# Scaling e in place of v^T e: the softmax factor in an attention and two-layer FFN kernel

## The chip, the cores and the metric

The kernel runs on one core of a Trainium2 chip. The metric is the device time of one execution in microseconds (us); the time before is the median of three runs. The profile is one further execution, taken by the hardware profiler.

## The reference, cut to what matters

All tensors are float32. The attention has 4 batches of 8 heads, 576 positions and a head size of 64:

```
scores = (q @ k^T) / 8
thresh = max(scores) - tau                       # per row
scores = where(scores >= thresh, scores, -1e9)
attn   = exp(scores - max(scores))
attn   = attn / (sum(attn) + 1e-9)               # per row
x      = attn @ v                                # heads joined: 2304 x 512
h      = ((x @ w1) * (x @ w2)) @ w3 @ w_out      # first FFN, 2304 x 512
g      = leaky_relu(h @ w_in, 0.01)              # 2304 x 2048
out    = g @ moe2_w_out                          # 2304 x 512
```

The change is to the line with the division by the sum.

## The kernel before, in words

The attention works on units: one pair of heads and one group of query rows. Group g=0 holds 256 query rows of the pair in two steps, g=1 holds 320 in three; a step is 128 rows of both heads, except the first of g=1, which takes the last 64 rows of both heads as one tile of 128. A batch is four units g=0 and then four units g=1; there are 32 units and 80 steps, and 64 of the steps hold two tiles of scores (128 query rows by 576 keys), 16 hold one.

A step goes through three functions. `scores` multiplies q by k into PSUM (tile sc), takes the row maximum on VectorE (nm) and writes e = exp(sc - max) on ScalarE. `mask` keeps e where the score is above the threshold, on VectorE (SCALAR_TENSOR_TENSOR), and gives the row sums in the same instruction (tile stat). `transposes` turns e on TensorE into PSUM (tp and, for the last 64 keys, tq) and copies it out to HH and tl. When a unit's steps are through, `weighted` multiplies v by HH and tl into a PSUM tile av: x transposed (64 numbers of each head of the pair in 128 partitions, query rows in the columns), without the division. ScalarE copies av to xs.

The query rows stand in the columns of av but in the partitions of the row sums. So `reciprocals` takes 1/(sum + 1e-9) on VectorE, GpSimd writes each factor 64 times side by side (rb), and `normalise` turns rb on TensorE into a PSUM tile bc (two transposes, and in g=1 one product more with the constant `pairs`), multiplies xs by bc on VectorE, and splits the result into a high part (ScalarE, rounded to the type fp32r) and a low part (GpSimd, the rest): x, the input of the first FFN. Products of the FFN take three passes over such parts.

The loop over steps n issues mask(n), scores(n+1), weighted of the unit before where one has just ended, and transposes(n), with pieces of other TensorE work in between: at first the folding of w3 and w_out (`fold_weights`, tile ps), later the first FFN of the queries that are through (`gated`: tiles psab, at, gt, psh), with 256 columns beside the g=1 units of the same batch and 320 beside the g=0 units of the next. `normalise` of a unit came in the second step of the next unit. Beside the first steps the weights are decoded from 64-bit words on ScalarE, VectorE and GpSimd (`stream`: tiles raw, t, lw). Behind the attention comes the second FFN, from about 650 us on.

TensorE's order and that of the DMA queue SP are as written in the code; ScalarE, VectorE and GpSimd are ordered by a scheduler, which also gives out the buffers of the pools. Pool ps_w has two PSUM banks, for av, bc, ps, psab, psh; sc0, sc1, tp and tq have one buffer each, and so a score tile must be masked before the next scores of that head can be computed.

Of the kernel before, what the change touches and what calls it, by code (L numbers as in the profile page):

```python
# [8 lines left out]
F32 = mybir.dt.float32  # L9
F32R = mybir.dt.float32r  # L10
# [3 lines left out]
ALU = mybir.AluOpType  # L14
# [29 lines left out]
def attention_gated_ffn(ctx: ExitStack, tc: tile.TileContext, qkv, tau, w3t, wout, w12, w2, out):  # L44
# [8 lines left out]
    def f(ap):  # L53
        return ap.bitcast(F32)
# [14 lines left out]

    ident = cpool.tile([P, P], F32, name="ident")  # L70
    make_identity(nc, ident)
    pairs = cpool.tile([P, D], F32, name="pairs")
    nc.vector.tensor_tensor(out=pairs, in0=ident[:, :D], in1=ident[:, D:], op=ALU.add)
    sides = cpool.tile([P, P], F32, name="sides")
    nc.vector.memset(sides, 0.0)
    nc.vector.memset(sides[:D, :D], 1.0)
    nc.vector.memset(sides[D:, D:], 1.0)
    qz = [apool.tile([P, P], F32, name=f"qz{i}") for i in range(2)]
    tl = [apool.tile([P, 2, 320], F32, name=f"tl{i}") for i in range(2)]
    for t in (*qz, *tl):  # L80
# [1 line left out]
    qzs = [apool.tile([P, 2, P], F32R, name=f"qzs{i}") for i in range(2)]  # L82
    for t in qzs:
        nc.vector.tensor_copy(t, tl[0][:, :, :P])
    one = cpool.tile([P, 1], F32, name="one")
    nc.vector.memset(one, 1.0)
    tauc = cpool.tile([P, 1], F32, name="tauc")
    neg = cpool.tile([P, 1], F32, name="neg")
    scl = cpool.tile([P, 1], F32, name="scl")
# [145 lines left out]
                    nc.vector.tensor_copy(qzs[u % 2][r, i, r], part[r, S:S + D])  # L235


    sc_t, e_t, stat = {}, {}, {}

    def scores(n):  # L240

# [34 lines left out]
    def mask(n):  # L276
        pair, g, c = STEPS[n]
        sc, ths = sc_t.pop(n)
        key = (pair, g)
        if key not in stat:  # L280
            stat[key] = apool.tile([P, 5], F32, tag="stat", name="stat", bufs=4)
        for a, th in enumerate(ths):
            ev = e_t[n][a].rearrange("p (a b) -> p a b", a=2)
            o = 4 if c is None else 2 * (c % 2) + a
            nc.vector.scalar_tensor_tensor(  # L285
                out=ev, in0=sc[a][:, :, :HS], scalar=th, in1=ev, op0=ALU.is_ge, op1=ALU.mult,
                accum_out=stat[key][:, o:o + 1])

    he_t = {}

# [32 lines left out]
                nc.scalar.copy(tail[D:, :, o:o + P], tq[D:])  # L323
            yield

    xs_t, x_t, rb_t = {}, {}, {}

    def weighted(pair, g):

        gw = GROUPS[g][1]  # L330
        vv = vv_t[units.index((pair, g))]
        HH, tail = he_t.pop((pair, g)), tl[pair % 2]
        av = ps_w.tile([P, 512], F32, tag="w", name="av")
        for i in range(NK):
            for a in (1, 0):
                kc = (4, 0, 1, 2, 3)[i]
                rhs = (HH[:, kc, a] if kc < 4 else tail[:, a])[:, :gw]
                nc.tensor.matmul(  # L338
                    av[a * D:a * D + D, :gw], vv[:, a, kc], rhs, start=(i == 0), stop=(i == NK - 1))
        xs = apool.tile([P, 320], F32, tag="xs", name="xs", bufs=2)  # L340
        nc.scalar.copy(xs[:, :gw], av[:, :gw])
        xs_t[pair, g] = xs

    def reciprocals(pair, g):

        st = stat.pop((pair, g))
        n = 4 + g
        rr = apool.tile([P, 5], F32, tag="rr", name="rr", bufs=2)
        nc.vector.tensor_scalar(out=rr[:, :n], in0=st[:, :n], scalar1=1e-9, scalar2=None, op0=ALU.add)
        nc.vector.reciprocal(rr[:, :n], rr[:, :n])  # L350
        rb = apool.tile([P, 3, P], F32, tag="rb", name="rb")
        nc.gpsimd.tensor_tensor(
            out=rb[:, :2].rearrange("p c (h d) -> p (c h) d", h=2),
            in0=rr[:, :4].unsqueeze(2).to_broadcast([P, 4, D]),
            in1=one.unsqueeze(2).to_broadcast([P, 4, D]), op=ALU.mult)
        if g:
            nc.gpsimd.tensor_tensor(
                out=rb[:, 2], in0=rr[:, 4:5].to_broadcast([P, P]), in1=sides, op=ALU.mult)
        rb_t[pair, g] = rb

    def normalise(pair, g):
        gq, gw, cs = GROUPS[g]
        xs, rb = xs_t.pop((pair, g)), rb_t.pop((pair, g))
        bc = ps_w.tile([P, 512], F32, tag="w", name="bc")
        if g:
            nc.tensor.matmul(bc[:, :D], rb[:, 2], pairs, start=True, stop=True)
        for i, c in enumerate(cs):
            nc.tensor.transpose(bc[:, Q0[c] - gq:Q0[c] - gq + P], rb[:, i], ident)  # L368
        nc.vector.tensor_tensor(out=xs[:, :gw], in0=xs[:, :gw], in1=bc[:, :gw], op=ALU.mult)  # L369
        x = xpool.tile([P, 2, 320], F32R, tag="x", name="x")  # L370
        nc.scalar.copy(x[:, 0, :gw], xs[:, :gw])
        nc.gpsimd.tensor_tensor(
            out=x[:, 1, :gw], in0=xs[:, :gw], in1=f(x[:, 0, :gw]), op=ALU.subtract)
        x_t[pair, g] = x


    wo_t, w3_t, w34_t, w12_t = {}, {}, {}, {}
# [116 lines left out]
    def run(gen, k):  # L494
        for _ in range(k):
            if next(gen, 0) == 0:
                return
# [15 lines left out]
    keep_busy(9)  # L513
    scores(0)
    keep_busy(10)
    weigh, norm = [], []
    filler = iter(())
    queue = []
    rate, due = 0.0, 0.0
    for n in range(NS):  # L520
# [29 lines left out]
        fill(1)  # L550
        for _ in pieces:
            pass
        if norm:
            normalise(*norm.pop())
        if last_of_unit:
            reciprocals(pair, g)
            weigh.append((pair, g))
        elif u and STEPS[n - 1][:2] != (pair, g):
            norm.append(units[u - 1])
        fill(2)  # L560
        if n < 3:
            keep_busy(7)
# [22 lines left out]
            filler = gated(b, gg)  # L585
            rate, due = (1.22, 1.55)[gg], 0.0
    weighted(*weigh.pop())
    run(filler, 2)
    normalise(B * 4 - 1, 1)
    s_att.close()  # L590


# [390 lines left out]
```

## Time and profile before

| | us |
|---|---|
| median of three runs | 1051.35 (1051.38, 1048.83, 1051.35) |
| profiled execution | 1048.59, span 1046.8 |
| TensorE busy, matmul | 1020.3 (97%) |
| TensorE busy, weight loads | 879.1 (84%) |
| VectorE busy | 579.3 (55%) |
| ScalarE busy | 546.8 (52%) |
| GpSimd busy | 288.2 (28%) |

In the rows, PE is TensorE's matmul and PEld its weight load, DVE is VectorE, ACT is ScalarE, POOL is GpSimd. L338 is line 338 of the kernel. `out<-in` names the tiles. Matmuls are pipelined: a row's length is from its start to its modelled end, and rows overlap, so the distance between the starts of weight loads tells better what one costs. A wait "A <- B" is idle time of engine A that ended when B was through.

### The profile page before, as it was taken

How to read it: one execution, taken by the hardware profiler on the slowest of the kernel's cores; microseconds unless marked ns; L12 is line 12 of the kernel's file. 1: busy time of each engine (PE TensorE's matmuls, PEld its weight loads, DVE VectorE, ACT ScalarE, POOL GpSimd, SP SyncE). 2: the span in 40 equal slices, each digit the busy share in tenths (PEclk: the TensorE clock that was granted, in tenths of full speed). 3: DMA queues.
4: the chain of work that ended last, by engine and by line, in shares of the span. 5: the costliest groups of instructions: out<-in, count | busy, mean ns of one | idle time of the engine just before them, and what ended most of it. 6: DMA issues, size and time to landing. Idle time of an engine off the chain costs nothing.

```text
span 1046.8 us, 17373 instructions
## 1 busy us (share of the span) xinstructions
PE 1020.3 (97%) x6632; PEld 879.1 (84%) x6632; DVE 579.3 (55%) x1269; ACT 546.8 (52%) x1052; POOL 288.2 (28%) x299
## 2 busy tenths in 40 slices
PE   7999799999999999999999999999989999999998
PEld 6554488889988898988898898999979999999997
DVE  7767867666676656776656736666572111621111
ACT  5767754454454544554544526688764333543332
POOL 3537712021211120211212126454551111411110
PEclk9999899999999999999999999999999999999999
DMA  9745321312111211212110223788975533045301
GB/s 317 251 158 159 113 60 40 104 32 72 43 52 58 62 32 55 59 40 71 44 50 20 69 86 130 277 314 317 358 277 183 203 141 134 1 151 207 151 1 61
DMA packets 42467, 129.58 MB, mean 124 GB/s; under 512 B 5520, under 2 KB 20880, under 8 KB 38032
## 3 DMA queue, kind: packets, MB, share of 16 engines
q1 hardware_dynamic: 42240, 128.47, 35.5%
q8 instruction: 52, 0.85, 0.3%
q14 instruction: 31, 0.25, 0.1%
q10 hardware_dynamic: 144, 0.00, 0.0%
HBM read 95.95 MB, written 32.51 MB: 123 GB/s over the span
## 4 chain that ended last, share of the span: by engine, by line
PE 88%; ACT 4%; DVE 3%; DMA 2%; issue 2%; POOL 1%; SPq 0%; POOLq 0%; ACTq 0%; DVEq 0%
PE po L896 18%; PE psab L439 17%; PE ps L861 17%; PE psh L458 10%; PE av L338 7%; PE sc L262 7%; PE tp L316 5%; PE ps L405 3%; PE tq L321 1%; DMA h3r<-h3d 1%; DVE t L152 1%; ACT e L271 1%; ACT t L149 1%; PE tp L305 1%; PE bc L368 1%
## 5 line engine op out<-in xcount | busy, mean ns | idle before, releaser
L439 PE MATMUL psab<-x,w 128*128 128x256 f32 (+1 forms) x1536 | 231.9, 302 | 0.0
L896 PE MATMUL po<-dn,gg 128*128 128x512 f32 x864 | 223.6, 391 | 0.0
L439 PEld LDWEIGHTS psab<-x,w 128*128 128x128 f32 x1536 | 208.7, 189 | 13.5 <-issue 9.5
L896 PEld LDWEIGHTS po<-dn,gg 128*128 128x128 f32 x864 | 160.3, 188 | 22.3
L861 PE MATMUL ps<-h,uph 128*128 128x384 f32 x672 | 173.1, 338 | 3.3 <-ACT snap L838 2.4
L271 ACT ACTIVATE e<-sc,nm 128x576 f32<-128x576 f32 x144 | 102.6, 742 | 87.5 <-DVE nm L269 87.3
L269 DVE TENSOR_REDUCE nm<-sc 128x1 f32<-128x576 f32 x144 | 103.2, 753 | 76.5 <-PE sc L262 76.5
L861 PEld LDWEIGHTS ps<-h,uph 128*128 128x128 f32 x672 | 123.6, 188 | 17.4 <-ACT snap L838 2.9
L843 DVE TENSOR_TENSOR sum<-snap,ps 128x384 f32<-128x384 f32 x72 | 39.8, 552 | 177.9 <-PE ps L861 162.9
L450 POOL TENSOR_TENSOR gt<-at,gt 128x256 fp32r<-128x256 f32 (+1 forms) x64 | 52.4, 819 | 270.0 <-ACT gt L449 269.8
L851 POOL TENSOR_TENSOR gg<-sum,gg 128x384 fp32r<-128x384 f32 x48 | 51.5, 1073 | 250.0 <-ACT gg L850 231.0
L285 DVE SCALAR_TENSOR_TENSOR e<-sc,th,e 128x576 f32<-128x576 f32 x144 | 113.8, 814 | 11.6 <-ACT e L271 11.1
L458 PE MATMUL psh<-gt,w 128*128 128x256 f32 (+1 forms) x768 | 115.5, 302 | 2.2 <-POOL gt L450 1.5
L861 PE MATMUL ps<-h,upl 128*128 128x384 f32 x336 | 113.4, 337 | 0.0
L458 PEld LDWEIGHTS psh<-gt,w 128*128 128x128 f32 x768 | 104.0, 189 | 7.7 <-issue 3.5
L316 PE MATMUL tp<-ident,e 128*128 128x128 f32 x512 | 77.8, 275 | 10.5 <-ACT HH L320 10.5
L838 ACT COPY snap<-ps 128x384 f32<-128x384 f32 x72 | 34.5, 479 | 98.5 <-PE ps L861 98.4
L316 PEld LDWEIGHTS tp<-ident,e 128*128 128x128 f32 x512 | 60.8, 141 | 20.2 <-ACT HH L320 13.0
L318 DVE COPY HH<-tp 128x512 f32<-128x512 f32 x64 | 44.1, 688 | 47.8 <-PE tp L316 47.0
L338 PE MATMUL av<-HH,vv 128*64 128x256 f32 (+1 forms) x512 | 67.5, 406 | 0.0
L405 PE MATMUL ps<-wo,w 128*128 128x512 f32 x128 | 60.8, 621 | 3.7 <-DVE xs L369 3.3
L848 ACT ACTIVATE sum<-sum 128x384 f32<-128x384 f32 x72 | 37.9, 526 | 49.6 <-DVE sum L843 49.6
(125 smaller groups left out, 1424.2 us busy)
## 6 DMA issues: line engine op xcount, KB each, us to landing
st<-in_w SPq DMA_DIRECT2D x40, 512.0 KB, 4.7
vv<-in_qkv SPq DMA_DIRECT2D x64, 160.0 KB, 2.3
dn<-dn_d SPq DMA_DIRECT2D x10, 1024.0 KB, 7.0
uph<-up_d SPq DMA_DIRECT2D x10, 896.0 KB, 8.1
upl<-up_d SPq DMA_DIRECT2D x10, 896.0 KB, 4.6
raw<-in_w3t SPq DMA_DIRECT2D x8, 1024.0 KB, 6.9
dn_d<-dn SPq DMA_DIRECT2D x8, 1024.0 KB, 7.6
up_d<-uph SPq DMA_DIRECT2D x8, 896.0 KB, 4.0
```

The costliest lines, as they stand in the source:

```text
L262: nc.tensor.matmul(sc[a][:, half, :HS], lhs, rhs, start=(i == 0), stop=(i == len(passes) - 1))
L269: nc.vector.tensor_reduce(out=nm, in_=sc[a][:, :, :HS], op=ALU.max, axis=AX.XY, negate=True)
L271: nc.scalar.activation(e[a].rearrange("p (a b) -> p a b", a=2), sc[a][:, :, :HS], AF.Exp, bias=nm)
L285: nc.vector.scalar_tensor_tensor(out=ev, in0=sc[a][:, :, :HS], scalar=th, in1=ev, op0=ALU.is_ge, op1=ALU.mult, accum_out=stat[key][:, o:o ...
L316: nc.tensor.transpose(tp[:, kc], e[a][:, kc * P:kc * P + P], ident)
L338: nc.tensor.matmul(av[a * D:a * D + D, :gw], vv[:, a, kc], rhs, start=(i == 0), stop=(i == NK - 1))
L405: nc.tensor.matmul(ps, w3_t[i][:, j * P:j * P + P], wo_t[j // 2][:, (j % 2) * 512:(j % 2) * 512 + 512], start=(j == 0), stop=(j == KF - 1))
L439: nc.tensor.matmul(ps[:, :gw], w12_t[i][:, a, mat * 512 + kk * P:mat * 512 + kk * P + P], xt[kk][:, c, :gw], start=(m == 0), stop=(m == 11))
L450: nc.gpsimd.tensor_tensor(out=gt[i][:, 1, :gw], in0=at[:, :gw], in1=f(gt[i][:, 0, :gw]), op=ALU.subtract)
L458: nc.tensor.matmul(ps[:, :gw], w34_t[i // 2][:, a, i % 2, o * P:o * P + P], gt[i][:, c, :gw], start=(m == 0), stop=(m == 23))
L861: nc.tensor.matmul(ps, (uph, upl)[a][:, wi, i * P:i * P + P], hs[k][:, c, i], start=(opens[k] and m == 0), stop=(m == 5), skip_group_check ...
L896: nc.tensor.matmul(po_t[o], gg[:, c, t * P:t * P + P], dn[:, i, a], start=(q == 0 and seen[o] == 1 and m == 0), stop=(q == NQ - 1 and seen ...
```

## The change

The row sums stand in the partitions of e, so e can be multiplied by a factor per partition. `mask` now adds 1e-9 to the sums, takes the reciprocal, and multiplies the masked e by it, in place: the last head's tile on VectorE, the other on ScalarE. v^T e then is x transposed, and `weighted` splits it into its two parts straight from the PSUM tile av, the high part on ScalarE and the low part on VectorE. `reciprocals`, `normalise`, the tiles xs, rb and bc and the constants are gone.

```diff
@@ mask
-        key = (pair, g)
-        if key not in stat:
-            stat[key] = apool.tile([P, 5], F32, tag="stat", name="stat", bufs=4)
+        st = apool.tile([P, 2], F32, tag="stat", name="stat", bufs=4)
         for a, th in enumerate(ths):
             ev = e_t[n][a].rearrange("p (a b) -> p a b", a=2)
-            o = 4 if c is None else 2 * (c % 2) + a
             nc.vector.scalar_tensor_tensor(
                 out=ev, in0=sc[a][:, :, :HS], scalar=th, in1=ev, op0=ALU.is_ge, op1=ALU.mult,
-                accum_out=stat[key][:, o:o + 1])
+                accum_out=st[:, a:a + 1])
+        m = len(ths)
+        nc.vector.tensor_scalar(out=st[:, :m], in0=st[:, :m], scalar1=1e-9, scalar2=None, op0=ALU.add)
+        nc.vector.reciprocal(st[:, :m], st[:, :m])
+        for a in range(m):
+            ev = e_t[n][a]
+            if a == m - 1:
+                nc.vector.tensor_scalar(out=ev, in0=ev, scalar1=st[:, a:a + 1], scalar2=None, op0=ALU.mult)
+            else:
+                nc.scalar.activation(ev, ev, AF.Copy, scale=st[:, a:a + 1])
@@ weighted
-        xs = apool.tile([P, 320], F32, tag="xs", name="xs", bufs=2)
-        nc.scalar.copy(xs[:, :gw], av[:, :gw])
-        xs_t[pair, g] = xs
-
-    def reciprocals(pair, g):
...
-    def normalise(pair, g):
...
-        bc = ps_w.tile([P, 512], F32, tag="w", name="bc")
-        if g:
-            nc.tensor.matmul(bc[:, :D], rb[:, 2], pairs, start=True, stop=True)
-        for i, c in enumerate(cs):
-            nc.tensor.transpose(bc[:, Q0[c] - gq:Q0[c] - gq + P], rb[:, i], ident)
-        nc.vector.tensor_tensor(out=xs[:, :gw], in0=xs[:, :gw], in1=bc[:, :gw], op=ALU.mult)
-        x = xpool.tile([P, 2, 320], F32R, tag="x", name="x")
-        nc.scalar.copy(x[:, 0, :gw], xs[:, :gw])
-        nc.gpsimd.tensor_tensor(
-            out=x[:, 1, :gw], in0=xs[:, :gw], in1=f(x[:, 0, :gw]), op=ALU.subtract)
-        x_t[pair, g] = x
+        x = x_t[pair, g] = xpool.tile([P, 2, 320], F32R, tag="x", name="x")
+        nc.scalar.copy(x[:, 0, :gw], av[:, :gw])
+        nc.vector.tensor_tensor(
+            out=x[:, 1, :gw], in0=av[:, :gw], in1=f(x[:, 0, :gw]), op=ALU.subtract)
@@ the loop over steps
-        if norm:
-            normalise(*norm.pop())
         if last_of_unit:
-            reciprocals(pair, g)
             weigh.append((pair, g))
-        elif u and STEPS[n - 1][:2] != (pair, g):
-            norm.append(units[u - 1])
```

VectorE in the first step of a g=0 unit of the second batch, before, from the mask of the next step's second head on (qkl is the low part of the q and k of the next unit):

```order
L285 SCALAR_TENSOR_TENSOR e_2083,stat_2065<-sc_2069,th_2090,e_2083 128x576
L229 TENSOR_TENSOR qkl_2096<-qk_1989,qkh_2095 128x832
L349 TENSOR_SCALAR rr_2265<-stat_2065 128x4
L350 RECIPROCAL rr_2265<-rr_2265 128x4
L447 TENSOR_TENSOR at_2125<-psab_2136,at_2125 128x320
L318 COPY HH_2127<-tp_2153 128x4x128
```

The same place now, in the unit after it:

```order
L274 SCALAR_TENSOR_TENSOR e_2295,stat_2397<-sc_2281,th_2302,e_2295 128x576
L221 TENSOR_TENSOR qkl_2308<-qk_2172,qkh_2307 128x832
L340 TENSOR_TENSOR x_2322<-av_2311,x_2322 128x256
L278 TENSOR_SCALAR stat_2397<-stat_2397 128x2
L279 RECIPROCAL stat_2397<-stat_2397 128x2
L283 TENSOR_SCALAR e_2295<-e_2295,stat_2397 128x576
L414 TENSOR_TENSOR at_2338<-psab_2349,at_2338 128x320
L316 COPY HH_2340<-tp_2366 128x4x128
```

The low part of x stands behind the split of the next unit, and the scaling of e ahead of the product at and of the copy HH.

TensorE at the last g=0 unit of the second batch, before, with what the instructions wait for (psab are products of the first FFN; two of them, for w1 and for w2, make one gt):

```order
L439 MATMUL psab_2562<-x_1332,w12_1071 128x320 [waits DVE_49]
L316 MATMUL tp_2579<-ident_82,e_2422 128x128 x4
L439 MATMUL psab_2586<-x_1332,w12_1071 128x320 [waits Activation_49]
L316 MATMUL tp_2603<-ident_82,e_2423 128x128 [waits Activation_49]
L439 MATMUL psab_2611<-x_1332,w12_1108 128x320 x3
L439 MATMUL psab_2649<-x_1332,w12_1108 128x320 [waits DVE_49]
```

The same place now:

```order
L406 MATMUL psab_2551<-x_1218,w12_1063 128x320 [waits DVE_49]
L314 MATMUL tp_2568<-ident_82,e_2418 128x128 [waits PE_49]
L406 MATMUL psab_2575<-x_1218,w12_1063 128x320 [waits Activation_49]
L314 MATMUL tp_2592<-ident_82,e_2419 128x128 [waits Activation_49]
L406 MATMUL psab_2600<-x_1218,w12_1100 128x320 [waits DVE_49]
L406 MATMUL psab_2643<-x_1218,w12_1100 128x320 [waits Activation_49]
```

Before, the four psab lie in the two banks of ps_w in turn; now all four lie in the same bank, so each waits until the one ahead of it is drained (psab_2551 and psab_2600 by ScalarE's copy at, psab_2575 by VectorE's product at). Over the whole program, two successive tiles of ps_w in TensorE's order have the same bank in one place before and in 25 places now: one in the g=1 units of the first batch, and in each later batch five in the g=0 units and three in the g=1 units.

TensorE in the second decoding, where the last weights are folded, before (sc_1130 are the next scores, psab_1139 the first product of the FFN):

```order
L316 MATMUL tp_1054<-ident_82,e_919 128x128 x4
L321 MATMUL tq_1040<-ident_82,e_919 128x128
L368 MATMUL bc_1062<-ident_82,rb_868 128x128 x2
L405 MATMUL ps34_1090<-wo_177,w3_697 128x512 x4
L405 MATMUL ps34_1090<-wo_308,w3_697 128x512 x4
L262 MATMUL sc_1130<-qk_775,qz1_94 128x288 x2
```

And now:

```order
L314 MATMUL tp_1053<-ident_82,e_912 128x128 x4
L319 MATMUL tq_1039<-ident_82,e_912 128x128
L372 MATMUL ps34_1082<-wo_169,w3_689 128x512 x4
L372 MATMUL ps34_1082<-wo_304,w3_689 128x512 x4
L254 MATMUL sc_1127<-qk_772,qz1_88 128x288 x2
```

The two transposes of rb are gone from between the transposes of e and the folding. Before, bc_1062 and ps34_1090 had the same bank.

## Rows read from the trace of the kernel before

**Rows 1.** Page, part 1: busy us, share of the span, instructions.

```profile
PE 1020.3 (97%) x6632; PEld 879.1 (84%) x6632; DVE 579.3 (55%) x1269; ACT 546.8 (52%) x1052; POOL 288.2 (28%) x299
```

**Rows 2.** Stretches: us, busy PE, PEld, DVE, ACT, POOL, granted clock, DMA, GB/s.

```profile
0.00:34.00 34.00, 26.86 (x171) 21.31 (x172) 26.19 (x68) 21.80 (x37) 12.88 (x16) 0.95 0.92 314
34.00:98.00 64.00, 64.00 (x265) 33.29 (x265) 40.84 (x88) 43.92 (x79) 32.89 (x28) 1.00 0.48 165
98.00:132.00 34.00, 27.44 (x119) 15.62 (x117) 28.02 (x49) 25.97 (x47) 25.66 (x22) 0.90 0.47 145
132.00:612.00 480.00, 476.30 (x3868) 421.12 (x3868) 315.30 (x787) 236.28 (x456) 87.19 (x124) 1.00 0.18 54
612.00:1047.00 435.00, 425.69 (x2216) 387.71 (x2212) 168.92 (x279) 218.81 (x435) 129.56 (x110) 1.00 0.48 178
```

**Rows 3.** Waits of PE, 132 to 612 us: us in total, times, longest.

```profile
PE tp L316 <- ACT HH L320: 3.2, 3, 1.1
```

**Rows 4.** Waits of PE, 0 to 34 us.

```profile
PE tp L316 <- ACT HH L320: 4.5, 3, 2.4
```

**Rows 5.** Waits of PE, 98 to 132 us.

```profile
PE ps L405 <- DVE xs L369: 3.3, 1, 3.3
PE tp L316 <- ACT HH L320: 2.8, 2, 2.2
```

**Rows 6.** Stretch 110 to 116 us, columns as in rows 2.

```profile
110.00:116.00 6.00, 5.45 (x7) 2.35 (x8) 4.48 (x6) 5.21 (x11) 6.00 (x7) 0.50 0.60 190
```

**Rows 7.** Order of time, weight loads: start us, us, engine, line, operation, tiles.

```profile
229.49 0.25 PEld L368 LDWEIGHTS bc<-ident,rb 128*128 128x128 f32 x2
229.78 0.30 PEld L439 LDWEIGHTS psab<-x,w 128*128 128x128 f32 x2
...
239.53 0.14 PEld L321 LDWEIGHTS tq<-ident,e 128*128 128x128 f32 x1
239.64 0.45 PEld L439 LDWEIGHTS psab<-x,w 128*128 128x128 f32 x3
...
299.56 0.30 PEld L366 LDWEIGHTS bc<-pairs,rb 128*128 128x128 f32 x2
...
299.95 1.49 PEld L439 LDWEIGHTS psab<-x,w 128*128 128x128 f32 x12
```

**Rows 8.** Order of time, draining of psab in a g=0 unit.

```profile
237.15 0.43 ACT L445 COPY at<-psab 128x320 f32<-128x320 f32 x1 [1.01 <-PE psab L439]
...
237.36 2.00 PE L439 MATMUL psab<-x,w 128*128 128x320 f32 x12
...
239.47 0.49 DVE L447 TENSOR_TENSOR at<-psab,at 128x320 f32<-128x320 f32 x1 [1.19 <-PE psab L439]
...
239.67 0.54 PE L439 MATMUL psab<-x,w 128*128 128x320 f32 x2
```

**Rows 9.** Groups by line and shape: busy us, mean ns of one, idle before.

```profile
L447 DVE TENSOR_TENSOR at<-psab,at 128x320 f32<-128x320 f32 x32 | 15.6, 488 | 23.8 <-PE psab L439 22.8 <-ACT at L445 1.0
...
L228 ACT CAST qkh<-qk 128x832 fp32r<-128x832 f32 x12 | 10.5, 876 | 0.0
...
L225 DVE TENSOR_SCALAR qk<-qk,scl 128x320 f32<-128x320 f32 x12 | 4.5, 377 | 0.0
L225 DVE TENSOR_SCALAR qk<-qk,scl 128x256 f32<-128x256 f32 x12 | 4.1, 345 | 0.0
...
L350 DVE RECIPROCAL rr<-rr 128x5 f32<-128x5 f32 x16 | 2.9, 184 | 0.1
```

**Rows 10.** Line 152, shifts of 128x512: ns min, median, max.

```profile
L152 DVE TENSOR_SCALAR t<-t x40: 414/706/1422, 11.0 to 125.5; 128x512 int32<-128x512 int32 x40
```

**Rows 11.** Order of time, second step of a g=1 unit.

```profile
293.07 1.08 DVE L229 TENSOR_TENSOR qkl<-qk,qkh 128x896 fp32r<-128x896 f32 x1
...
294.08 0.39 DVE L235 CAST qzs<-qkh 64x64 fp32r<-64x64 f32 x2
...
297.05 0.46 PEld L316 LDWEIGHTS tp<-ident,e 128*128 128x128 f32 x4
```

More of the change, by code (lines that the diff above doesn't have):

```diff
@@ L71, in attention_gated_ffn @@
     make_identity(nc, ident)
[L72 to L77, printed above, removed]
     qz = [apool.tile([P, P], F32, name=f"qz{i}") for i in range(2)]
@@ L84, in attention_gated_ffn @@
         nc.vector.tensor_copy(t, tl[0][:, :, :P])
-    one = cpool.tile([P, 1], F32, name="one")
-    nc.vector.memset(one, 1.0)
     tauc = cpool.tile([P, 1], F32, name="tauc")
@@ L235, in split_unit @@
                     nc.vector.tensor_copy(qzs[u % 2][r, i, r], part[r, S:S + D])
-    sc_t, e_t, stat = {}, {}, {}
+    sc_t, e_t = {}, {}
     def scores(n):
@@ L324, in transposes @@
             yield
-    xs_t, x_t, rb_t = {}, {}, {}
+    x_t = {}
     def weighted(pair, g):
@@ L339, in weighted @@
                     av[a * D:a * D + D, :gw], vv[:, a, kc], rhs, start=(i == 0), stop=(i == NK - 1))
-        xs = apool.tile([P, 320], F32, tag="xs", name="xs", bufs=2)
-        nc.scalar.copy(xs[:, :gw], av[:, :gw])
-        xs_t[pair, g] = xs
-    def reciprocals(pair, g):
[L346 to L351, printed above, removed]
-        nc.gpsimd.tensor_tensor(
-            out=rb[:, :2].rearrange("p c (h d) -> p (c h) d", h=2),
-            in0=rr[:, :4].unsqueeze(2).to_broadcast([P, 4, D]),
-            in1=one.unsqueeze(2).to_broadcast([P, 4, D]), op=ALU.mult)
-        if g:
-            nc.gpsimd.tensor_tensor(
-                out=rb[:, 2], in0=rr[:, 4:5].to_broadcast([P, P]), in1=sides, op=ALU.mult)
-        rb_t[pair, g] = rb
-    def normalise(pair, g):
-        gq, gw, cs = GROUPS[g]
-        xs, rb = xs_t.pop((pair, g)), rb_t.pop((pair, g))
-        bc = ps_w.tile([P, 512], F32, tag="w", name="bc")
-        if g:
-            nc.tensor.matmul(bc[:, :D], rb[:, 2], pairs, start=True, stop=True)
-        for i, c in enumerate(cs):
-            nc.tensor.transpose(bc[:, Q0[c] - gq:Q0[c] - gq + P], rb[:, i], ident)
-        nc.vector.tensor_tensor(out=xs[:, :gw], in0=xs[:, :gw], in1=bc[:, :gw], op=ALU.mult)
-        x = xpool.tile([P, 2, 320], F32R, tag="x", name="x")
-        nc.scalar.copy(x[:, 0, :gw], xs[:, :gw])
-        nc.gpsimd.tensor_tensor(
-            out=x[:, 1, :gw], in0=xs[:, :gw], in1=f(x[:, 0, :gw]), op=ALU.subtract)
-        x_t[pair, g] = x
+        x = x_t[pair, g] = xpool.tile([P, 2, 320], F32R, tag="x", name="x")
+        nc.scalar.copy(x[:, 0, :gw], av[:, :gw])
+        nc.vector.tensor_tensor(
+            out=x[:, 1, :gw], in0=av[:, :gw], in1=f(x[:, 0, :gw]), op=ALU.subtract)
     wo_t, w3_t, w34_t, w12_t = {}, {}, {}, {}
@@ L515, in attention_gated_ffn @@
     keep_busy(10)
-    weigh, norm = [], []
+    weigh = []
     filler = iter(())
@@ L587, in attention_gated_ffn @@
     weighted(*weigh.pop())
-    run(filler, 2)
-    normalise(B * 4 - 1, 1)
     s_att.close()
```

## The prediction

> **What bounds the kernel now.** I read the busy shares first, then the stretches, then TensorE's waits in each stretch, and last the order of time at three places. TensorE is busy for 97% of the span, VectorE and ScalarE for 55% and 52% [rows 1]. By stretches the picture splits [rows 2]. From 34 to 98 us TensorE has no gap at all, and from 132 to 612 us it is busy for 476 of 480 us while VectorE has 165 us and ScalarE 244 us to spare; its longest sum of waits there is 3.2 us, on the copies of HH [rows 3]. In these two stretches, and in the last one, an instruction less on TensorE is time gained, and an instruction more on VectorE or ScalarE costs nothing while it stays beside TensorE's work. Two stretches are different: 0 to 34 us (start, decoding of weights) and 98 to 132 us (decoding of w1 and w2). There VectorE is busy for 26 and 28 of 34 us, and TensorE waits: for HH 4.5 us in the first [rows 4], and 3.3 us for the product xs (a PSUM bank that bc holds) and 2.8 us for HH in the second [rows 5]. After that second wait the granted clock stood at 0.50 from 110 to 116 us, its lower level (1.2 GHz) [rows 6].
>
> **The change part by part.**
>
> *TensorE loses the transposes of the factors.* What one normalise costs TensorE is the distance from its first weight load to the next product's. Without it a product follows the tq transpose by 0.11 us; with it the first bc load stands at just that distance, and the product comes 0.29 us later in a g=0 unit and 0.39 us later in a g=1 unit [rows 7]. Sixteen units of each kind: 16 x 0.29 + 16 x 0.39 = 10.9 us less. All but one of these places lie in stretches where TensorE is the bound (three in 34 to 98, twenty-seven in 132 to 612, one behind 612); one lies in the second decoding.
>
> *PSUM banks.* v^T e now keeps its bank until two readers are through, ScalarE for the high part and VectorE for the low part. The order of VectorE in the section on the change puts the low part behind the split of the next unit's q and k; the pool answers this by giving the bank of a finished psab to the next psab in 25 places, where two banks alternated before. TensorE then can't start the next product until the earlier one is drained. Price of one, from a g=0 unit [rows 8]: ScalarE's copy at ended at 237.58 and the next product started at 237.36, so 0.22 us would be lost; VectorE's product at ended at 239.96 against 239.67, 0.29 us. With the signal on top I take 0.3 us for either. Each batch from the second on has four of these two kinds (three of the first, one of the second) and four with score products between, which I put at nothing, since the drain fits beside them. So 3 x 4 x 0.3 = 3.6 us more.
>
> *What mask adds.* Per step one add and one reciprocal on two numbers, 0.18 us each by the reciprocal of before [rows 9]; one scaling of 128x576 on VectorE, and in 64 of 80 steps one on ScalarE. The like on VectorE took 0.345 us at 256 and 0.377 us at 320 columns, 0.5 ns for each further column, so 0.50 us at 576. Its bounds are 0.41 us (the fastest 512-column shift) and 1.42 us (the slowest one, beside GpSimd's decoding) [rows 9, 10]. I take 0.50 us, because the nearest row has the same operands. On ScalarE the cast of 832 columns took 0.876 us [rows 9]; 576/832 of it is 0.61 us, 0.876 us is the upper end, and I take 0.70 us. So 0.86 us of VectorE a step, and the low part of x, 0.49 us a unit by the product at of the same width [rows 9], which GpSimd did before.
>
> *Where that is hidden.* From 132 to 612 us there are 68 steps and 27 units: 68 x 0.86 + 27 x 0.49 = 72 us on VectorE against 165 us idle, even without what it loses. But a queue is in order, so the narrowest place counts. That is the g=1 unit's second step: behind the split at 293.07 stand two pairs of casts of 0.39 us each, then (new) the low part of x, add and reciprocal, then ScalarE's scaling: 293.07 + 1.08 + 0.78 + 0.49 + 0.36 + 0.70 = 296.5, and TensorE transposes that tile at 297.05 [rows 11]. It fits with 0.57 us to spare. What is queued behind (the next reductions on VectorE) moves by about 1 us and meets a wait for scores there. I cost it at nothing; if the cover is gone, each microsecond there is 16 us in all. In a g=0 step more products stand between the mask and the transposes.
>
> *The start.* In the first four steps TensorE does nothing but scores, transposes and filling, and VectorE is nearly full. There 4 x 0.86 = 3.4 us more stand in the chain from mask to the next scores, because the next q's scaling and reductions are queued behind. Bounds: nothing, if all hides in the 7.8 us that VectorE idles, and 4 x (0.36 + 1.42) = 7.1 us.
>
> *The second decoding.* The 3.3 us for xs go, since no bc holds a bank. Were TensorE not to fall idle so long, up to 3 of the 6 us at the lower clock would come back as well; the wait for HH stays, so I count half, 1.5 us. Against it, three steps with 0.86 us more on a nearly full VectorE: 2.6 us, of which I count half, 1.3 us. Together 3.5 us less; bounds 6.3 us less and, with 1.78 us a step and only the wait gone, 2.0 us more.
>
> *Sum:* -10.9 + 3.6 + 3.4 - 3.5 = -7.4 us. The profiled execution took 1048.59 us (span 1046.8), which would become 1041.2. The three timed runs lie at 1048.83, 1051.38 and 1051.35, so the profiled one is 2.8 us under their median; on the median the sum gives 1043.95 us, and I predict 1044.
>
> **The rivals.**
>
> *The decoding eats it (no change).* The shift of 128x512 on VectorE, one of the kind that the scaling is, took 0.41 us at its fastest and 0.71 us in the median, 1.42 us at most, all in the stretches where GpSimd decodes [rows 10]. If the scalings of the early steps fare like the slowest, the start costs 7.1 us and the second decoding 2.0 us: -10.9 + 3.6 + 7.1 + 2.0 = +1.8, 1053.2 us on the median. For it: VectorE is that full in both stretches. Against it: TensorE's stretch from 34 to 98 us can swallow lateness of the decoding. The Trainium skill states the mechanism (SBUF — State Buffer, section Who interferes with whom): a VectorE copy or scaling from SBUF to SBUF in a two-port mode and a GpSimd instruction exclude each other, and the later one waits for the whole of the earlier. The spread of those shifts agrees with it, and by that rule this rival is the case wherever GpSimd is at work when a scaling comes.
>
> *The banks cost more (slower).* The 25 successions take back the whole gain once their mean wait is (3.6 + 7.4) / 25 = 0.44 us instead of 0.14, and the kernel is slower by more than 0.3% from 0.57 us. The way there: the drain stands behind a scaling on its engine (0.70 us, and 0.1 us for what I priced), 25 x 0.8 = 20 us instead of 3.6, so -7.4 + 16.4 = +9.0, 1060 us. For it: the copies at stand in the same ScalarE queue as the scalings, and those wait for a reciprocal. Against it: in the order after, the scaling stands behind the copy of the same piece of work, and ScalarE was idle for 1.01 us ahead of that copy [rows 8].
>
> *More is gained.* The start hides its share, the second decoding gives all of 6.3 us, the bank waits are half as long: -10.9 + 1.8 - 6.3 = -15.4, 1036 us. For it: the wait for xs and the lower clock hang together. Against it: VectorE has nearly no gap at the start.
>
> **How the numbers follow.** Forecast 0.53, no change 0.20, slower 0.13, more gained 0.14. A measurement of this kernel tells about 0.3% (3.15 us) from nothing. Faster by more: 0.45 of the forecast's 0.53, and 0.14, in round numbers 0.60; slower by more 0.15 (the slower rival and some of the no-change case); the rest, 0.25, the same. The forecast's own range, from its bounds, is 1039 to 1049 us; the range that holds 8 of 10 reaches down to the larger gain and up past the no-change case, 1036 to 1055 us.
>
> **What would show it.** In the profile after: no bc rows, and TensorE's product 0.11 us behind tq where bc stood; waits of psab for ScalarE's copy at or VectorE's product at in the batches from the second on, 0.3 us each, some twelve of them; no wait of ps for xs in the second decoding; the stretch without gaps beginning about 3 us later than at 34 us; scalings of 0.5 us on VectorE from 132 us on and longer ones before. The prediction is wrong if TensorE waits for scaled tiles e between 132 and 612 us, if the bank waits are near 0.6 us or there are 25 of them, or if 34 us and 132 us are reached later than now by more than 7 and 4 us.

## The result, and the profile after

The changed kernel takes 1042.49 us (median of six runs, 1041.12 to 1043.32), the kernel before, beside it, 1051.37 us (six runs, 1048.83 to 1052.86): ratio 0.9918, 95% interval 0.9903 to 0.9933. That is 8.9 us less, and 1.5 us under the 1044 of the prediction. The profiled executions differ by less: 1048.59 us before, 1042.57 us now, 6.0 us. All that follows is read from these two; the profiled one of before lies at the fast end of its runs, with a mean granted clock of 0.995 where its runs at the medians of the sets below show 0.992, and what they do in the other 2.9 us no trace shows.

The totals fit; the stages don't. Matching each weight load of TensorE with the same one of before (the bc loads left out) gives the time that a stage won or lost (minus is won):

| stage, up to the start of | before, us | now, us | change in the stage | by the prediction's terms |
|---|---|---|---|---|
| first folding product ps | 33.76 | 36.24 | +2.5 | +3.4 |
| v^T e of the fifth unit, behind the second decoding | 127.74 | 127.74 | -2.5 | -4.7 |
| v^T e of the last unit | 609.56 | 607.33 | -2.2 | -5.7 |
| first product of the second FFN | 663.75 | 658.13 | -3.4 | -0.4 |
| last product | 1042.59 | 1036.57 | -0.4 | 0 |

Page of the changed kernel, part 1, which answers to [rows 1]:

```profile
PE 1013.0 (97%) x6536; PEld 871.3 (84%) x6536; DVE 635.7 (61%) x1440; ACT 575.6 (55%) x1084; POOL 237.9 (23%) x219
```

Its stretches, with the columns of [rows 2]:

```profile
0.00:34.00 34.00, 24.29 (x158) 19.57 (x159) 28.07 (x68) 21.58 (x36) 11.18 (x14) 0.95 0.86 295
34.00:98.00 64.00, 63.55 (x269) 33.18 (x267) 45.73 (x104) 46.64 (x82) 27.52 (x22) 1.00 0.47 162
98.00:132.00 34.00, 28.69 (x124) 17.33 (x120) 29.32 (x52) 28.37 (x51) 26.68 (x20) 0.90 0.52 171
132.00:612.00 480.00, 474.80 (x3801) 415.42 (x3800) 363.98 (x942) 261.67 (x484) 43.95 (x55) 1.00 0.19 55
```

VectorE has 56 us more in all, 49 of them from 132 to 612 us; the granted clock of 98 to 132 us is 0.90 as before.

TensorE's weight loads at a place where two bc loads stood [rows 7], and at the last g=0 unit of the second batch, where four psab share a bank (what stands in brackets is idle time before the row, and what ended it):

```profile
229.83 0.14 PEld L319 LDWEIGHTS tq<-ident,e 128*128 128x128 f32 x1
229.94 1.17 PEld L406 LDWEIGHTS psab<-x,w 128*128 128x128 f32 x8
...
237.38 0.14 PEld L319 LDWEIGHTS tq<-ident,e 128*128 128x128 f32 x1
237.79 1.76 PEld L406 LDWEIGHTS psab<-x,w 128*128 128x128 f32 x12 [0.26 <-ACT at L412]
...
239.98 0.14 PEld L319 LDWEIGHTS tq<-ident,e 128*128 128x128 f32 x1
240.47 1.17 PEld L406 LDWEIGHTS psab<-x,w 128*128 128x128 f32 x8 [0.35 <-DVE at L414]
```

Without bc the product stands 0.11 us behind tq. In a shared bank it stands 0.41 and 0.49 us behind, and the idle time ends with ScalarE's copy at (line 412) and VectorE's product at (line 414): the bank costs 0.30 and 0.38 us.

Waits of TensorE from 98 to 132 us (in total, times, longest), answering to [rows 5], and the stretch 121 to 128 us:

```profile
PE psab L406 <- DVE w L378: 4.0, 1, 4.0
PE tp L314 <- ACT HH L318: 1.3, 1, 1.3
```

```profile
121.00:128.00 7.00, 6.23 (x27) 4.99 (x29) 6.26 (x14) 6.10 (x12) 5.59 (x5) 0.54 0.00 1
```

The wait of ps for xs is gone, and a new one has come some 11 us later: a psab waits 4.0 us until the bank of the last ps34 is drained, last by VectorE (w, line 378). Behind it the clock is at its lower level, as it was behind the old one [rows 6]. The drain, in order of time (the last ps34, ScalarE's copy out of it, the VectorE instruction ahead of VectorE's part, and that part):

```profile
107.83 7.03 PE L372 MATMUL ps<-wo,w 128*128 128x512 f32 x16
...
119.15 0.58 ACT L377 CAST w<-ps 128x512 fp32r<-128x512 f32 x1
119.37 1.75 DVE L152 TENSOR_TENSOR w<-lw,w 128x512 fp32r<-128x512 f32 x1 [1.16 <-POOL lw L150]
...
121.04 0.68 DVE L378 TENSOR_TENSOR w<-ps,w 128x512 fp32r<-128x512 f32 x1
```

The products end at 114.86 us. ScalarE's copy starts 4.3 us later, behind seven instructions of the decoding with 0.2 us of idle time in all between them, and VectorE's part another 1.3 us after that copy's end, behind one. So the drain is late in ScalarE's queue first, and in VectorE's second.

A g=1 unit of the first batch, VectorE in order of time, and the scores that wait for it:

```profile
137.82 0.51 DVE L278 TENSOR_SCALAR stat<-stat 128x2 f32<-128x2 f32 x1
138.36 0.17 DVE L279 RECIPROCAL stat<-stat 128x2 f32<-128x2 f32 x1
138.56 0.52 DVE L283 TENSOR_SCALAR e<-e,stat 128x576 f32<-128x576 f32 x1
139.00 0.68 DVE L316 COPY HH<-tp 128x512 f32<-128x512 f32 x1
139.60 0.52 DVE L199 TENSOR_SCALAR qz<-qk,scl 64x64 f32<-64x64 f32 x2
140.17 0.78 PEld L254 LDWEIGHTS sc<-qk,qz 128*128 128x128 f32 x4 [0.81 <-DVE qz L199]
```

Add, reciprocal, scaling and, behind them, the copy HH stand ahead of qz. Before, it began right behind the mask:

```profile
136.75 0.81 DVE L285 SCALAR_TENSOR_TENSOR e<-sc,th,e 128x576 f32<-128x576 f32 x1
...
137.49 0.93 DVE L207 TENSOR_SCALAR qz<-qk,scl 64x64 f32<-64x64 f32 x2
```

The end of the attention, before: waits of TensorE's weight loads from 605 to 665 us, and SP's DMAs of those microseconds. h3d<-ht stores the first FFN's result, h<-h3d reads it for the second FFN, st<-in_w loads the second FFN's weights:

```profile
PEld psh L458 <- POOL gt L450: 2.0, 2, 1.2
PEld psh L458 <- ACT gt L449: 0.9, 1, 0.9
```

```profile
605.64 10.71 SPq L466 DMA_DIRECT2D h3d<-ht  x3
616.45 2.76 SPq L745 DMA_DIRECT2D h<-h3d  x6
...
636.76 5.19 SPq L628 DMA_DIRECT2D st<-in_w  x3
```

The same now; no wait of psh is left:

```profile
603.42 3.72 SPq L433 DMA_DIRECT2D h3d<-ht  x2
607.19 4.84 SPq L705 DMA_DIRECT2D h<-h3d  x6
...
627.04 5.25 SPq L588 DMA_DIRECT2D st<-in_w  x3
```

The loads of h no longer stand behind the third store and start 9 us earlier. So do the loads of the second FFN's weights, and their decoding no longer falls on the last at and gt of the first FFN. Beside `normalise`, the change takes out the line ahead of it at the end of the attention, `run(filler, 2)` (two pieces of the first FFN), which the diff in the section on the change doesn't show.

### The profile page after: what moved, and what is told of

Read it like the earlier page. It is cut to its first block, busy times and chain, and to the rows that moved or that the text cites. A ratio compares the mean times of both kernels' runs of the same rounds, so it can differ in the third digit from the quotient of the medians.

```text
span 1040.8 us, 17334 instructions
## 1 busy us (share of the span) xinstructions
PE 1013.0 (97%) x6536; PEld 871.3 (84%) x6536; DVE 635.7 (61%) x1440; ACT 575.6 (55%) x1084; POOL 237.9 (23%) x219
## 4 chain that ended last, share of the span: by engine, by line
PE 89%; DVE 5%; ACT 2%; DMA 1%; issue 1%; POOL 0%; SPq 0%; DVEq 0%; ACTq 0%; POOLq 0%
PE psab L406 20%; PE po L856 19%; PE ps L821 17%; PE psh L425 10%; PE av L336 7%; PE sc L254 7%; PE tp L314 5%; PE ps L372 3%; PE tq L319 1%; DVE nm L261 1%; DMA h3r<-h3d 1%; DVE e L274 1%; DVE t L144 1%; DVE e L283 1%; PE tp L303 1%
## 5 line engine op out<-in xcount | busy, mean ns | idle before, releaser
L274 DVE SCALAR_TENSOR_TENSOR e<-sc,th,e 128x576 f32<-128x576 f32 x144 | 113.9, 814 | 10.9 <-ACT e L263 10.4
L821 PEld LDWEIGHTS ps<-h,upl 128*128 128x128 f32 x336 | 63.6, 189 | 0.0
```

Source lines behind the costliest of these rows:

```text
L274: nc.vector.scalar_tensor_tensor(out=ev, in0=sc[a][:, :, :HS], scalar=th, in1=ev, op0=ALU.is_ge, op1=ALU.mult, accum_out=st[:, a:a + 1])
L821: nc.tensor.matmul(ps, (uph, upl)[a][:, wi, i * P:i * P + P], hs[k][:, c, i], start=(opens[k] and m == 0), stop=(m == 5), skip_group_check ...
```

## The experiments

Each median stands beside runs of the kernel before in the same set: 1050.49 us for 1 to 4, 1050.96 for 5 to 8, 1051.21 for 9 to 11. One trace was kept of each kernel, and kernels with the same program up to a place reach it at times that differ: the folding starts 0.6 us later in 4 than in the kernel before and 2.6 us later in 8 than in the changed kernel, and the fifth unit's product comes 1.0 us later in 6 than in 3. Differences between single traces ahead of 132 us are no surer than that.

| | median, us | ratio to before, 95% interval |
|---|---|---|
| changed kernel | 1042.49 | 0.9918, 0.9903 to 0.9933 |
| 1 no scaling | 1039.30 | 0.9891, 0.9877 to 0.9904 |
| 2 one reader of the bank | 1042.29 | 0.9927, 0.9913 to 0.9942 |
| 3 q and qz first | 1038.64 | 0.9889, 0.9876 to 0.9902 |
| 4 before, last normalise earlier | 1047.03 | 0.9968, 0.9956 to 0.9980 |
| 5 before without factors | 1038.88 | 0.9889, 0.9873 to 0.9904 |
| 6 as 3, parts of x on GpSimd | 1037.34 | 0.9876, 0.9862 to 0.9890 |
| 7 as 6, high part on ScalarE | 1038.09 | 0.9882, 0.9868 to 0.9896 |
| 8 decoding off GpSimd | 1044.06 | 0.9933, 0.9919 to 0.9947 |
| 9 as 3, early scaling on ScalarE | 1039.60 | 0.9891, 0.9873 to 0.9908 |
| 10 as 6, g=0 units alone | 1035.60 | 0.9852, 0.9838 to 0.9865 |
| 11 as 9 and 10 | 1036.20 | 0.9858, 0.9845 to 0.9872 |

**1. The changed kernel without the scaling.** It leaves out the division.

```diff
-        nc.vector.tensor_scalar(out=st[:, :m], in0=st[:, :m], scalar1=1e-9, scalar2=None, op0=ALU.add)
-        nc.vector.reciprocal(st[:, :m], st[:, :m])
-        for a in range(m):
...
```

Expected:

> The changed kernel without the add, the reciprocal and the two scalings of e (the division is left out); banks and TensorE's order stay as they are, 25 successions in one bank included. Theory: the scaling costs what the weight loads of TensorE lose in places where no bank and no bc stands: about 2.4 us before the first folding (36 us), 1.5 us in the g=1 units of the first batch (scores wait for qz, which stands behind the scaling on VectorE), and some 0.13 to 0.16 us in four places of each later batch. The first product v^T e behind the second decoding (127.74 us before and after) is set by the decoding itself and comes at most 0.7 us earlier. Sum: 0.7 + 1.5 + 1.7 = 4 us less than the changed kernel, 1038 to 1039 us. Rival A (the scaling is hidden everywhere, as the prediction had it for 132 to 612 us, and the start's loss is taken up by the decoding): within 1 us of the changed kernel, 1042. Rival B (the second decoding is held up by the scaling): the product at 127.74 comes 2.4 us earlier or more, and the kernel gains 6 us, 1036.

Measured: 1039.30 us. By the weight loads the folding starts 2.4 us earlier than in the changed kernel, at 33.83 us, which is where it was before the change; the fifth unit's product 3.8 us earlier, at 123.90; the two waits for qz (0.88 and 0.66 us) and six steps of 0.14 to 0.16 us at transposes are gone. So the scaling costs at the places that the theory named, and in the second decoding it costs 1.4 us more, as rival B had it; the theory, by which that stage would swallow most of the start's 2.4 us, fell there. The medians differ by 3.2 us, the profiled spans (1035.3 and 1040.8 us) by 5.5; the profiled execution of this kernel took 1037.16 us, 2.1 under its median, so the steps may overstate the whole.

**2. One reader of the bank: ScalarE copies to xs, GpSimd makes the low part.**

```diff
-        nc.scalar.copy(x[:, 0, :gw], av[:, :gw])
-        nc.vector.tensor_tensor(
-            out=x[:, 1, :gw], in0=av[:, :gw], in1=f(x[:, 0, :gw]), op=ALU.subtract)
+        xs = apool.tile([P, 320], F32, tag="xs", name="xs", bufs=2)
+        nc.scalar.copy(xs[:, :gw], av[:, :gw])
+        nc.scalar.copy(x[:, 0, :gw], xs[:, :gw])
+        nc.gpsimd.tensor_tensor(
+            out=x[:, 1, :gw], in0=xs[:, :gw], in1=f(x[:, 0, :gw]), op=ALU.subtract)
```

Expected:

> The changed kernel, but ScalarE copies v^T e to xs in SBUF first and the two parts are made from xs, the low part on GpSimd: the PSUM bank has one reader. The two banks now alternate everywhere (no succession in one bank, 25 in the changed kernel). Theory: the waits of psab in the later batches go (three times 0.28 us and one of 0.38 us a batch, of which 0.22 us came back at the following psh: 1.02 us a batch, 3.1 us), and VectorE has 0.45 us a unit less; 3 us less than the changed kernel, 1039.5 us. Rival A (these steps are not the banks but work of VectorE that stands in the way): the steps stay and the time stays within 1 us, 1042. Rival B (ScalarE's 0.43 us copy more in each unit delays exp and HH): up to 32 x 0.2 us of new waits of the transposes for HH, no gain or 2 us slower, 1042 to 1045.

Measured: 1042.29 us. Theory and rival B are both there: in each later batch the psab lose steps of 0.28, 0.29, 0.29 and 0.38 us, and transposes that wait for HH get 0.37, 0.28 and 0.28 us; 1.6 us more are lost up to the fifth unit. The waits of the banks are real, and removing them so brings nothing: from the fifth unit to the last 1.8 us are won, and 1.6 lost ahead of it.

**3. q and qz ahead of the scaling.**

```diff
+    def factor(n):          # add, reciprocal and scalings, out of mask
...
         mask(n)
         if last_of_unit:
             scale_unit(u + 1)
+        factor(n)
```

Expected:

> The changed kernel with the add, the reciprocal and the scalings issued behind the scaling of the next unit's q (and of qz), so that VectorE prepares the next scores first and scales e afterwards; banks as in the changed kernel. Theory: in the g=1 units of the first batch the scores no longer wait for qz (0.88 and 0.66 us after other steps), 1.5 us less, 1041 us; the start may gain up to 1 us as well, since there too the next q stands behind the scaling. Rival (the transposes wait for the later scaling instead): the same loss appears as waits of tp for e, and the time stays within 0.5 us of the changed kernel.

Measured: 1038.64 us, 3.9 us less than the changed kernel. VectorE in the same g=1 unit:

```profile
136.74 0.94 DVE L199 TENSOR_SCALAR qz<-qk,scl 64x64 f32<-64x64 f32 x2
137.71 0.35 DVE L204 TENSOR_SCALAR qk<-qk,scl 128x256 f32<-128x256 f32 x1
137.98 0.16 DVE L282 TENSOR_SCALAR stat<-stat 128x2 f32<-128x2 f32 x1
```

The steps of 0.88 and 0.66 us are gone, as expected. The folding starts 0.5 us and the fifth unit's product 2.0 us earlier, the latter more than expected. No transpose waits for e. (The trace wins 2.0 us up to the fifth unit and 1.5 at qz, of which 0.6 are lost again right behind the fifth unit's product.)

**4. The kernel before, with the last normalise earlier.**

```diff
     weighted(*weigh.pop())
-    run(filler, 2)
     normalise(B * 4 - 1, 1)
```

Expected:

> The kernel before, with the last unit's normalise right behind its product, no two pieces of the FFN between them; nothing else. With that, SP's order has six of the loads of h for the second FFN ahead of the third store of the first FFN's result, as in the changed kernel; before they stood behind it. Theory: the 3 us of waits of psh for gt at 650 to 653 us come from this: the loads of h started at 616.45 us, 9 us later than in the changed kernel, so the decoding of the second FFN's weights fell on the last at and gt of the first FFN. Expected: loads of h near 610 us, no waits of psh between 640 and 660 us, and 3 us less than before, 1048.4 us. Rival A (the order on SP doesn't matter; the waits go because GpSimd and ScalarE have no low part and no xs): the waits stay, 1051.4 us. Rival B: the waits go, but the second FFN's first products wait as long instead: 1051 us.

Measured: 1047.03 us, 3.5 us less than before. The three steps at psh, 1.25, 0.99 and 0.86 us, go, and SP starts the loads of h earlier:

```profile
606.07 3.73 SPq L466 DMA_DIRECT2D h3d<-ht  x2
610.87 3.83 SPq L744 DMA_DIRECT2D h<-h3d  x6
```

The same three steps (1.25, 0.98 and 0.86 us) are in the trace of the changed kernel. So 3.1 us of its gain come from two pieces of work that no longer stand ahead of the last unit's `normalise`, and not from the factors.

**5. The kernel before without factors.** It leaves out the division, GpSimd's rb included.

```diff
...
-        bc = ps_w.tile([P, 512], F32, tag="w", name="bc")
...
-            nc.tensor.transpose(bc[:, Q0[c] - gq:Q0[c] - gq + P], rb[:, i], ident)
-        nc.vector.tensor_tensor(out=xs[:, :gw], in0=xs[:, :gw], in1=bc[:, :gw], op=ALU.mult)
```

Expected:

> The kernel before without reciprocals, rb, bc and the product (the division is left out): x is split from xs as before, on ScalarE and GpSimd; the two banks alternate everywhere. Theory: what TensorE loses is worth its distance in the rows: 0.22 to 0.29 us in each of 16 g=0 units and 0.39 us in each of 16 g=1 units, 10.4 us; the wait for xs in the second decoding (3.3 us) goes as well, and since no scaling of e takes it back, the first product v^T e behind the decoding comes about 4 us earlier than at 127.74 us, as in the changed kernel without scaling (123.90). 10.4 + 3 = 13.4 us less than before, 1037 us, and up to 3 us less still where the order on SP (here three of the six loads of h ahead of the third store) spares the waits of psh at 650 us: 1034 to 1037. Rival (the transposes of bc filled gaps that TensorE has anyway): no steps of 0.3 to 0.4 us at those places, under 6 us in all, above 1044 us.

Measured: 1038.88 us; the transposes did cost. From the second unit on, 31 places have a step each: 0.22 us three times, then 0.39 to 0.40 us in g=1 units and 0.22 to 0.30 us in g=0 units, 10.2 us in all. At psh 2.5 of 3.1 us go as well. But the second decoding gains nothing here: the folding is done 6.2 us earlier, and then a psab waits (waits of the weight loads, 98 to 132 us):

```profile
PEld psab L424 <- DVE w L396: 5.4, 1, 5.4
```

The fifth unit's product starts at 128.27 us (127.74 before), where I expected 124. In this kernel TensorE's wait for xs was not what ends the stage; when it goes, the drain of ps34 is late next, here too on ScalarE first (its copy starts 5.0 us behind the last product). With the decoding's 3 to 4 us missing, the median is 2 us above the upper end of what I expected.

From the fourth unit's product v^T e to the fifth's, the stage with the second decoding, it took 42.46 us before, 42.21 in this kernel, 40.63 in the changed one, 39.20 in experiment 1 and 39.11 in 3. So with the wait for xs gone the stage wins 0.2 us where ScalarE still copies av to xs and GpSimd makes the low part of x, and 3.3 us where x is split straight from av and no scaling stands in the way (1) or it stands behind q (3).

**6 and 7. As 3, and both parts of x from xs on GpSimd from the fifth unit on (6), or the high part on ScalarE (7).**

```diff
+        if units.index((pair, g)) < 4:
+            ...          # both parts straight from av, as in the changed kernel
+            return
+        xs = apool.tile([P, 320], F32, tag="xs", name="xs", bufs=2)
+        nc.scalar.copy(xs[:, :gw], av[:, :gw])
+        nc.gpsimd.tensor_copy(x[:, 0, :gw], xs[:, :gw])      # 7: nc.scalar.copy
```

Expected (6):

> The changed kernel with q and qz ahead of the scaling (as in the run before), and from the fifth unit on with one reader of the PSUM bank: ScalarE copies v^T e to xs, and GpSimd makes both parts from xs. The banks alternate everywhere. Theory: the waits of psab in the later batches go, 1.02 us a batch, and since ScalarE has no more copies than the changed kernel, no new waits of the transposes for HH come: 1038.64 - 3.1 = 1035.6 us. Rival (GpSimd's 1.8 us a unit more stands ahead of the low part of gt or slows VectorE): waits of psh for gt or longer products on VectorE, no gain, 1038 to 1040.

Expected (7):

> As the kernel with both parts on GpSimd, but ScalarE makes the high part from xs, one copy of 0.43 us a unit more on ScalarE. Theory: what kept the copy to xs from gaining was this copy: it stands ahead of HH and brings back the steps of 0.28, 0.28 and 0.37 us a batch at the transposes: 0.9 us a batch, 2.8 us more than the kernel with both parts on GpSimd, 1038.4 us. Rival (those steps came from xs in the first batch and the start, or from GpSimd): the same time as the kernel with both parts on GpSimd, within 0.7 us.

Measured: 1037.34 and 1038.09 us. The bank steps go in both (1.24 us a batch), and in 6 two transposes a batch in g=1 units get 0.43 us each; in 7 they get 0.28 us each and a third transpose 0.37 us. So ScalarE's extra copy is not the only cause. The medians lie 1.3 and 0.6 us under that of 3, which the intervals leave open, and 6 can't be told from 7; the trace of 6 has lost 1.0 us against 3 ahead of the first unit that it changes.

**8. All low parts of the decoded w1 and w2 on VectorE.**

```diff
-                    eng = nc.vector if by_dve and c else nc.gpsimd
+                    eng = nc.vector if by_dve else nc.gpsimd
```

Expected:

> The changed kernel with all low parts of the decoded w1 and w2 on VectorE (0.68 us each) and none on GpSimd (1.3 to 1.6 us each), where they alternated. Theory: the second decoding is paced by VectorE's queue, in which the scaling of e also stands: the first product behind it comes 2 to 4 us later than at 127.74 us and the kernel is as much slower, 1044.5 to 1046.5 us. Rival (GpSimd paces it; it is busy for 6.0 of 6 us at 116 to 122 us): that product comes 1 to 3 us earlier, 1040 to 1041.5 us.

Measured: 1044.06 us, 1.6 us above the changed kernel, with intervals that overlap. The fifth unit's product starts at 131.03 us, 3.3 us later, and psab waits 6.6 us for w. But 2.6 of the 3.3 us are there when the folding starts, at 38.86 us, ahead of the first instruction that the edit changes (at about 90 us); the stage from the fourth to the fifth unit takes 41.30 us, 0.7 more than in the changed kernel, and the profiled execution took 1046.58 us, 2.5 above the median. That the product fell in the range of the theory is luck. What the run does show is that GpSimd alone doesn't pace this stage: it is busy for 18.7 us from 98 to 132 us where it was for 26.7, and nothing is won. That VectorE's queue paces it is not shown, the less so as ScalarE's copy of the last ps34 starts 5.8 us behind the last product here.

**9, 10, 11. As 3, with both scalings on ScalarE in the first four units (9); as 6, but in the g=0 units of the later batches alone (10); both (11).**

```diff
-            if a == m - 1:
+            if a == m - 1 and units.index((pair, g)) >= 4:      # 9, 11
...
-        if units.index((pair, g)) < 4:
+        if g or units.index((pair, g)) < 4:                     # 10, 11
```

Expected (9):

> The changed kernel with q and qz ahead of the scaling, and in the first four units (13 steps with two tiles or less, beside the decoding) both tiles scaled on ScalarE, none on VectorE; from the fifth unit on as before. Theory: VectorE paces these stages, where one scaling took 0.8 to 1.2 us on it in the mean beside GpSimd's work; without nine of them the first folding starts about 1 us earlier (35.71 us in the run with q first) and the first product behind the second decoding 2 us earlier (125.70): 1036.6 us. Rival (ScalarE is as full there, and its 0.78 us a scaling stand ahead of exp and HH): the folding starts no earlier or later and the time stays within 1 us of 1038.6 us.

Expected (10):

> The changed kernel with q and qz ahead of the scaling; one reader of the bank (copy to xs on ScalarE, both parts on GpSimd) only in the g=0 units of the later batches, two readers in the g=1 units. Ten successions in one bank are left (25, and none with one reader everywhere). Theory: in the run with one reader everywhere the 1.24 us a batch won at the psab were given back as 0.43 us at each of two transposes that wait for HH in the g=1 units, because ScalarE's and VectorE's chain from scores to HH there had no more slack; that doesn't depend on who reads v^T e, so the same steps come again: 1037.3 us, within 0.7 us. Rival (the steps came from GpSimd's work in the g=1 units): they go, and the time is 1035 us.

Expected (11):

> Both together: q and qz ahead of the scaling, ScalarE alone scales in the first four units, one reader of the bank in the g=0 units of the later batches. If both gains stand and lie in different stages, they add up: 1038.6 - 2 - 1.3 = 1035.3 us. If the first is nothing, 1037.3 us.

Measured: 1039.60, 1035.60 and 1036.20 us. In 9 the folding starts 0.9 us and the fifth unit's product 0.7 us earlier than in 3, not 2 us, and the median shows no gain: inconclusive. In 10 my theory fell, and what the rival expected came: the steps go. TensorE's waits from 132 to 612 us, in 6 and in 10:

```profile
PE tp L318 <- ACT HH L322: 5.0, 9, 1.0
```

```profile
PE tp L318 <- ACT HH L322: 3.1, 3, 1.0
```

With xs in the g=1 units left out, the six waits for HH are gone, while the bank steps (0.28, 0.29, 0.29, 0.38 us in each later batch) stay away: 3.7 us less than 3 in the trace, 3.0 in the median. Which part of xs made those waits, the other order of VectorE's queue or GpSimd's work, I didn't separate. 10 is the fastest kernel here, 6.9 us under the changed one; 11 adds nothing that can be told from it.

## Why the prediction was right, and where its steps were not

- *The transposes, -10.9 us:* right. 10.2 us over 31 places (experiment 5); the three early g=0 ones, and one in each later batch, are worth 0.22 and not 0.29 us.
- *The banks, +3.6 us:* right, in place and size: twelve waits of 0.28 to 0.38 us, 1.24 us a batch, 3.7 us; experiment 10 takes them away and gains as much. The other thirteen successions, put at nothing, show no step above 0.13 us.
- *The start, +3.4 us:* right in kind, 2.4 us by one trace each (experiment 1). All nine kernels with a scaling start the folding later (34.81 to 38.86 us) than the four without (33.76 to 34.33).
- *The second decoding, -3.5 us:* mis-sized; 1.8 us were won (the 2.5 of the table less three transposes at 0.22). The sum was 3.3 for xs and 1.5 for the clock, less 1.3 for the scaling. The scaling's part was right (1.4, experiment 1). The step that failed is that nothing would be late behind the wait for xs: without scaling the stage wins 3.3 us (experiment 1) and not 4.8, because the drain of the last ps34 is late next, 4.0 us in the changed kernel, and the clock falls behind that wait (0.90 in the stretch, as before). Experiment 5 shows that even these 3.3 us aren't the price of the wait alone: with ScalarE's copy to xs and GpSimd's low part left in, its end is worth 0.2 us. What makes that difference no run separates; ScalarE's queue is the first in which the drain is late.
- *Scalings of 132 to 612 us hidden, 0:* wrong by about 2 us: 2.5 us by the steps of experiment 1, of which some come back at other places, so that 1.8 us are left at the last unit. I looked for the narrowest place in a later batch and found the margin there ([rows 11]; TensorE loads that tile at 297.13 now, without a wait for e). The narrowest place was in the first batch, where qz isn't split and stands behind the mask in the queue: 1.5 us (experiments 1 and 3). Six more steps of 0.14 to 0.16 us went with the scaling in experiment 1; at one of them (281.8 us) a transpose waits for HH, which stands on ScalarE behind an exp that is 1.1 us later. "I cost it at nothing" held for e itself and not for what is queued behind it.
- *Not in the sum:* 3.1 us at 650 us (experiment 4). I followed `normalise` and not the two pieces of the first FFN that stood ahead of it at the end and went too, nor the DMAs queued behind them.
- *Durations:* the scaling on VectorE 0.52 us (0.50 taken), on ScalarE 0.78 (0.70 taken), the low part of x 0.42 and 0.49 us.

So the total came out near because terms missed on both sides, and that is luck: 1.7 too much from the decoding, 0.7 too much from the transposes and about 2 too little cost of the scaling, against 1.0 of the start and 3.1 at the end; about 1 us more, lost from 132 to 612 us, is placed nowhere. The 7.4 us less of the sum lie between the 6.0 of the profiled executions and the 8.9 of the medians. Of the rivals, none came about as a whole. That the decoding eats the gain was half true: up to 127.7 us nothing of it is left, and six of the first twelve scalings were stretched as the shifts of [rows 10] were (last section). The slower one, a drain behind a scaling, did not come: from 132 us on no bank wait is above 0.38 us, and the one of 4.0 us ahead of that stands behind the decoding.

## What to carry to other kernels

Before a wait of the bounding engine is booked as a gain, follow the queues of the other engines to the next thing that it wants from any of them; here a wait of 3.3 us gave way to one of 4.0 us, and its end was worth 3.3 us in one kernel and 0.2 in another. Work added to an in-order queue is hidden only if what stands behind it is: look at each kind of place where the queue differs (the first batch, the start), and put what the bounding engine needs next ahead of the new work, here worth 3.9 us (experiment 3). And compare what the end of a phase no longer waits for; two pieces of work there moved the loads of the next stage by 9 us and its time by 3.1.

## What the runs showed of the hardware

The scaling on VectorE takes 0.51 to 0.52 us, or much longer. In the first 130 us of the changed kernel six of twelve took 0.98 to 1.63 us, and each of the six ended 0.31 to 0.33 us behind the end of a GpSimd instruction whose row starts within 0.25 us of its own (two of them 0.03 and 0.04 us later). A seventh, whose row starts 0.07 us ahead of GpSimd's, took 0.52 us, and GpSimd's instruction 1.58 us where most of its kind took 1.27. One of the six, and one with GpSimd idle:

```profile
51.58 1.27 POOL L147 TENSOR_TENSOR w<-t,lw 128x512 int32<-128x512 int32 x1 [0.57 <-DVE stat L278]
```

```profile
51.75 1.42 DVE L283 TENSOR_SCALAR e<-e,stat 128x576 f32<-128x576 f32 x1
63.03 0.52 DVE L283 TENSOR_SCALAR e<-e,stat 128x576 f32<-128x576 f32 x1
```

The common end speaks for a wait and not for a slower run: a scaling here costs 0.5 us, or the rest of GpSimd's instruction and 0.3 us. By the Trainium skill (SBUF — State Buffer, section Who interferes with whom) a scaling in a two-port mode and a GpSimd instruction block each other for the whole of the one that is first. The trace agrees but for the end: a whole scaling behind GpSimd's would end 0.52 us after it, and the rows show 0.31 to 0.33; why, no run here shows.

In the second FFN one wait of TensorE, for the tile snap, was followed by a stretch at the lower clock, about 3.4 us in the changed kernel, in some kernels and not in others. It took 3.5 us in the changed kernel (granted clock 0.72 from 770 to 776 us), 3.7 in experiment 1 and 3.2 in 10, all with the lower clock behind; in the kernel before TensorE waited 2.4 and then 0.9 us there, in experiment 3 2.8 and 0.9, and the clock stayed at 1.00. The length of the wait alone doesn't tell the two apart: experiment 7 waited 3.3 and 0.8 us there and stayed at 1.00. This moves such kernels by about 1 us against each other, though the code of this stage is the same in all of them.
